# Laying one batch's attention as a row of ticks between half-steps of another batch's MoE

## The chip, the cores and the metric

The kernel runs on one core of a Trainium2 chip. The metric is the device time of one execution in microseconds (us). The kernel before takes 290.18 us (median of three runs, 288.84 to 292.52). A profile of one execution gives a span of 288.6 us from the first to the last instruction; all windows and rows below come from it.

## The reference: what is computed

Eight batches (B), eight heads, 576 positions (S), head width 64. First an attention without a score matrix, then a mixture of experts in which a whole batch goes to one expert:

```python
q_s = softmax(q, axis=-1)                     # over the 64 columns of a row
k_s = softmax(k, axis=2)                      # over the 576 positions
kv  = einsum('bhsd,bhse->bhde', k_s, v)       # 64 x 64 per head
x   = einsum('bhsd,bhde->bhse', q_s, kv)      # then laid as B x S x 512
pooled = x.mean(axis=1); logits = pooled @ w_gate       # one row of 8 per batch
e = argmax(logits); gate = softmax(logits)[e]
out[b] = gate * (relu(x[b] @ w1[e]) @ w2[e])  # 512 -> 1024 -> 512
```

The exact softmaxes subtract the maximum and add 1e-9 to the sum; the kernel leaves both out for q and k, whose values are small. With the inputs used here the eight batches choose the experts 2, 3, 3, 1, 3, 3, 4 and 6.

## The kernel before

Each batch is worked on in two halves of four heads (n = 0 to 15). A half loads q, k and v (three tiles of 128 x 1152, 576 KB each), takes exps on ScalarE, casts v on GpSimd, sums and scales q, and then runs through TensorE in the steps KV, T (twice), X (twice). After two halves the batch has its input X to the MoE, kept transposed in `xt`, and a gate step picks the expert and starts the transfer of its weights into one of five slots, unless another slot holds them already. Later a "fetch" on VectorE copies the slot that holds the weights into the batch's own slot (onto itself where they were just loaded).

```python
BUFS = {"mm": 3, "ht": 1, "kv": 2, "t": 1, "x": 1}     # PSUM: eight banks of 128 x 512 fp32
def bank(tag):
    return psum.tile([128, 512], FP32, name=tag, tag=tag, bufs=BUFS[tag])

def prepare_half(n):                       # all at one place in the order
    nc.scalar.activation(out=eq, in_=q, func=Exp)
    nc.scalar.activation(out=ek, in_=k, func=Exp)
    nc.gpsimd.tensor_copy(out=va, in_=v)
    nc.vector.tensor_reduce(out=qs, in_=eq, op=add)
    nc.vector.reciprocal(out=qsi, in_=qs)
    eng = nc.vector if n < 4 else nc.gpsimd
    eng.tensor_tensor(out=eq, in0=eq, in1=qsi, op=mult)
    load_half(n + 3)

def attention(b):                          # a generator: 12 steps per batch
    for i in range(2):
        kps = [bank("kv") for g in range(2)]
        # ... KV: 18 matmuls into kps[g][:, 0:129]; VectorE scales them into kvs[g]
        yield
        for g in range(2):
            tp = bank("t")                 # batch 0: "mm" for g == 1
            # ... T: nine transposes of eq into tp
            nc.vector.tensor_copy(out=qt, in_=tp)
            yield
        for g in range(2):
            px, pxt = bank("x"), kps[g][:, 192:256]       # 512 and 64 columns
            # ... X: one matmul into each
            nc.vector.tensor_tensor_reduce(out=xt[:, c, 0:512], in0=px, ..., accum_out=pooled)
            nc.vector.tensor_tensor_reduce(out=xt[:, c, 512:576], in0=pxt, ..., accum_out=pooled)
            yield
    # ... gate: pooled @ w_gate into bank("x"), argmax, DMAs of w1 and w2 on GpSimd's queue
    nc.vector.tensor_single_scalar(out=nmx, in_=mx8[:, 0:1], scalar=-1.0, op=mult)
    nc.scalar.activation(out=ex, in_=zz, func=Exp, bias=nmx, accum_out=sm)
    yield
    # ... VectorE: gt = 1 / sm, hl = gt in two fp16 parts; TensorE spreads hl over 128 partitions
    yield

def moe(b):                                # a generator: 13 units
    for fc in range(8):
        # ... H: 4 matmuls of 512 columns into bank("mm"), 4 of 64 into "ht"; ScalarE: ReLU to hsb
        yield
    for st in range(4):
        # ... O: 8 matmuls of 512 columns into bank("mm"); ScalarE: osb = gate * po; DMA out
        yield
    # ... tail: 16 matmuls of 256 columns
    yield
```

The order of the instructions on each engine is the order of the program. Attention is run ahead: 18 attention steps before the first MoE, then 1.25 steps after every MoE unit, and `fetch(b-1)` of w1 and of w2 stand at steps 6 and 8 of batch b.

Of the kernel before, what the change touches and what calls it, by code (L numbers as in the profile page):

```python
# [9 lines left out]
FP32 = mybir.dt.float32  # L10
FP16 = mybir.dt.float16
U32 = mybir.dt.uint32
AF = mybir.ActivationFunctionType
ALU = mybir.AluOpType
# [5 lines left out]
def kernel(  # L20
# [40 lines left out]
    BUFS = {"mm": 3, "ht": 1, "kv": 2, "t": 1, "x": 1}  # L61

    def bank(tag):
        return psum.tile([128, 512], FP32, name=tag, tag=tag, bufs=BUFS[tag])

# [39 lines left out]
    def pair_src(t, b, i):  # L105

        return t[b].rearrange("(i n g) (p j) d -> i (g p) n (j d)", i=2, n=2, p=64)[i]
# [5 lines left out]
    def load_half(n):  # L113
        if n >= 2 * B:
            return
        b, i = divmod(n, 2)
        ins[n] = {}
        for name, t in (("q", q), ("k", k), ("v", v)):
            x = in_pool.tile([128, 2, J * Dh], FP32, name=f"{name}_in")
            nc.sync.dma_start(out=x, in_=pair_src(t, b, i))  # L120
            ins[n][name] = x.rearrange("p n (j d) -> p n j d", j=J)

    def prepare_half(n):
        t = ins.pop(n)
        eq = e_pool.tile([128, J, 2, Dh], FP16, name="eq")
        nc.scalar.activation(out=eq.rearrange("p j n d -> p n j d"), in_=t["q"], func=AF.Exp)  # L126
        ek = e_pool.tile([128, J, 2, Dh], FP16, name="ek")
        nc.scalar.activation(out=ek.rearrange("p j n d -> p n j d"), in_=t["k"], func=AF.Exp)  # L128
        va = v_aug[n % NVB]
        nc.gpsimd.tensor_copy(out=va[:, :, 1:].rearrange("p j (n d) -> p n j d", n=2), in_=t["v"])  # L130
        qs = stat.tile([128, J, 2], FP32, name="qs")
        nc.vector.tensor_reduce(out=qs, in_=eq, op=ALU.add, axis=AX.X)  # L132
        qsi = stat.tile([128, J, 2], FP32, name="qsi")
        nc.vector.reciprocal(out=qsi, in_=qs)  # L134
        eng = nc.vector if n < 4 else nc.gpsimd
        eng.tensor_tensor(  # L136
            out=eq, in0=eq, in1=qsi.unsqueeze(3).to_broadcast([128, J, 2, Dh]), op=ALU.mult,
        )
        halves[n] = (eq, ek, va)
        load_half(n + 3)  # L140

    def attention(b):
        roomy = b == 0
        xt = xt_pool.tile([128, ND, S], FP16, name="xt")
        pooled = gat_pool.tile([128, ND], FP32, name="pooled")
        for i in range(2):
            eq, ek, va = halves.pop(2 * b + i)
            kps = [bank("kv") for g in range(2)]
            for j in range(J):
                for g in range(2):  # L150
                    r = slice(64 * g, 64 * g + 64)
                    nc.tensor.matmul(  # L152
                        kps[g][:, 0:129], lhsT=ek[r, j], rhs=va[r, j],
                        start=(j == 0), stop=(j == J - 1),
                    )
            kvs = []
            for g in range(2):
                icv = kv_pool.tile([128, 1], FP32, name="icv")
                nc.vector.reciprocal(out=icv, in_=kps[g][:, 0:1])  # L159
                kv = kv_pool.tile([128, 128], FP16, name="kv")  # L160
                nc.vector.scalar_tensor_tensor(
                    out=kv, in0=kps[g][:, 1:129], scalar=icv, in1=blkmask, op0=ALU.mult, op1=ALU.mult,
                )
                kvs.append(kv)
            yield
            qts = []
            for g in range(2):
                r = slice(64 * g, 64 * g + 64)
                tp = bank("mm" if roomy and g == 1 else "t").bitcast(FP16)
                for j in range(J):  # L170
                    nc.tensor.transpose(  # L171
                        out=tp[:, 64 * j:64 * j + 64], in_=eq[r, j], identity=ident[r, r],
                    )
                qt = qt_pool.tile([128, S], FP16, name="qt")
                nc.vector.tensor_copy(out=qt, in_=tp[:, 0:S])  # L175
                qts.append(qt)
                yield
            for g in range(2):
                c = 2 * i + g
                px = bank("mm" if roomy and g == 1 else "x")  # L180
                pxt = kps[g][:, 192:256]
                nc.tensor.matmul(px, lhsT=kvs[g], rhs=qts[g][:, 0:SM], start=True, stop=True)  # L182
                nc.tensor.matmul(pxt, lhsT=kvs[g], rhs=qts[g][:, SM:S], start=True, stop=True)  # L183
                nc.vector.tensor_tensor_reduce(  # L184
                    out=xt[:, c, 0:SM], in0=px, in1=ones_f32.to_broadcast([128, SM]),
                    scale=1.0, scalar=0.0, op0=ALU.mult, op1=ALU.add, accum_out=pooled[:, c:c + 1],
                )
                nc.vector.tensor_tensor_reduce(
                    out=xt[:, c, SM:S], in0=pxt, in1=ones_f32.to_broadcast([128, ST]),
                    scale=1.0, scalar=pooled[:, c:c + 1], op0=ALU.mult, op1=ALU.add,  # L190
                    accum_out=pooled[:, c:c + 1],
                )
                yield
# [13 lines left out]
        cond, sidx = None, None  # L207
# [40 lines left out]
        seqs[b] = [xt, None, sidx]  # L248
        nmx = gat_pool.tile([1, 1], FP32, name="nmx")
        nc.vector.tensor_single_scalar(out=nmx, in_=mx8[:, 0:1], scalar=-1.0, op=ALU.mult)  # L250
        ex = gat_pool.tile([1, E], FP32, name="ex")
        sm = gat_pool.tile([1, 1], FP32, name="sm")
        nc.scalar.activation(out=ex, in_=zz, func=AF.Exp, bias=nmx, accum_out=sm)
        yield
        gt = gat_pool.tile([1, 1], FP32, name="gt")
        nc.vector.reciprocal(out=gt, in_=sm)

        hl = gat_pool.tile([1, 2], FP16, name="hl")
        nc.vector.tensor_copy(out=hl[:, 0:1], in_=gt)
        nc.vector.tensor_scalar(  # L260
            out=hl[:, 1:2], in0=hl[:, 0:1], scalar1=gt, scalar2=-2048.0, op0=ALU.subtract, op1=ALU.mult
        )
        pb = bank("x")
        nc.tensor.matmul(pb[:, 0:2], lhsT=ones_row, rhs=hl, start=True, stop=True)
# [3 lines left out]
        seqs[b][1] = gate  # L268
        yield

    def fetch(b, w_all):

        sidx = seqs[b][2]
        if sidx is None:
            return
        s_val = nc.values_load(
            sidx[0:1, 0:1], engines=[ET.DVE], min_val=0, max_val=NS - 1,
            skip_runtime_bounds_check_because=IN_RANGE,
        )
        nc.vector.tensor_copy(  # L280
            out=w_all[:, b % NS], in_=w_all[:, ds(s_val, 1)].rearrange("p o c f -> p (o c) f")
        )

    def moe(b):
        xt, gate, _ = seqs[b]
# [22 lines left out]
        for st in range(4):  # L308
            po = bank("mm")
            for fc in range(NF):  # L310
                nc.tensor.matmul(  # L311
                    po, lhsT=hsb[:, fc, st * 128:st * 128 + 128], rhs=w2_sb[:, fc, :],
                    start=(fc == 0), stop=(fc == NF - 1),
                )
            osb = o_pool.tile([128, D], FP32, name="osb")
            nc.scalar.mul(osb, po, gate)  # L316
            for jj in range(2):
                nc.sync.dma_start(out=out_p[b, :, 2 * st + jj], in_=osb[64 * jj:64 * jj + 64])
            yield
# [16 lines left out]

    NA = 12
    att = {}
    pos = [0]
    prepared = [0]  # L340

    def att_step():

        if pos[0] >= NA * B:
            return False
        b, s = divmod(pos[0], NA)
        half_now = min(2 * b + (1 if s >= 1 else 0) + (1 if s >= 6 else 0), 2 * B - 1)
        while prepared[0] <= half_now:
            prepare_half(prepared[0])
            prepared[0] += 1  # L350
        if b not in att:
            att[b] = attention(b)
        if b and s == 6:
            fetch(b - 1, w1_all)
        if b and s == 8:
            fetch(b - 1, w2_all)
        next(att[b])
        pos[0] += 1
        return True

    for n in range(3):
        load_half(n)
        if n == 0:
            load_wg()
    with tc.manual_schedule(engines={ET.PE, ET.DVE, ET.Activation, ET.Pool, ET.SP}):
        for _ in range(NA + 6):
            att_step()
        owed = 0.0
        for b in range(B):
            for m, _ in enumerate(moe(b)):  # L370
                owed = min(owed + 1.25, NA * (b + 3) - pos[0])
                while owed >= 1.0:
                    att_step()
                    owed -= 1.0
                if m == 10 and b + 1 < B:
                    while pos[0] < NA * (b + 2):
                        att_step()
            if b == B - 2:
                fetch(B - 1, w1_all)
                fetch(B - 1, w2_all)  # L380
# [30 lines left out]
```

The softmax here doesn't subtract the row's maximum and nothing guards it: scores larger than these inputs give would overflow.

## Time and profile before

| what | value |
|---|---|
| median time, span of the profile | 290.18 us, 288.6 us |
| first MoE matmul | 39.94 us |
| the last two MoEs, with no attention inside | 15.85 and 15.91 us |
| granted TensorE clock, mean over the span | 0.887 |
| DMA queue 1 (inputs, outputs), share of 16 engines | 40.3% |
| DMA queue 0 (weights), share of 16 engines | 22.7% |

A row of a group or of the order of time names the source line, the engine, the operation, and output <- input by the program's names, with partitions x elements and type. "x9" is a count. In the order of time the first number is the start and the second the length in us; a bracket holds the idle time of that engine just before and what ended it. A row of waits names the engine and line that waited, what it waited for, the total in us, the number of times and the longest. PEld is the load of TensorE's stationary operand, which overlaps the matmuls. Line L171 is the transposes, L175 the copy of their result, L182 X, L184 its reading, L264 the spreading of the gate, L280 the slot copy, L293 and L311 the two MoE matmuls, L132 the sum for q.

### The profile page before, as it was taken

To read this page: it belongs to the slowest core of one execution; us is meant where nothing else is said; L and a number is where in the kernel's file an instruction comes from. 1 tells how busy PE (TensorE), PEld (TensorE's weight loads), DVE (VectorE), ACT (ScalarE), POOL (GpSimd) and SP (SyncE) were. 2 spreads that over 40 slices of the span, in tenths; PEclk is the share of its full clock that TensorE was granted. 3 is DMA by queue.
4 is the path that set the end of the run, shared out by engine and by line. 5 is a ranking of instruction groups with operands and counts; after the bars stand their busy time and mean duration, and the time that the engine had idled before them with its cause. 6 is when DMAs were issued, how large, how long until landed. Compare 5 with 4: busy or idle time off the path is not lost.

```text
span 288.6 us, 4585 instructions
## 1 busy us (share of the span) xinstructions
PE 197.5 (68%) x1608; PEld 102.6 (36%) x1608; DVE 132.5 (46%) x416; ACT 105.0 (36%) x161; POOL 68.0 (24%) x89
## 2 busy tenths in 40 slices
PE   0242376667577296673796649959289688899992
PEld 0230243433344142441353323534134444454541
DVE  2677745553756842448514574143841447211000
ACT  4330214255045222541334511453124523454641
POOL 1310742371114205332014020140206200500000
PEclk9999997999599787995997966986759959999999
DMA  7999899499917726997156261410007950798324
GB/s 234 395 391 392 225 242 313 115 191 294 374 44 242 249 53 130 189 313 267 38 121 213 74 214 31 98 36 2 0 0 141 219 98 0 146 222 164 93 49 116
DMA packets 28791, 48.55 MB, mean 168 GB/s; under 512 B 3168, under 2 KB 10336, under 8 KB 28768
## 3 DMA queue, kind: packets, MB, share of 16 engines
q1 hardware_dynamic: 19456, 37.76, 40.3%
q0 software_dynamic: 8736, 10.49, 22.7%
q8 instruction: 12, 0.20, 0.3%
q10 hardware_dynamic: 576, 0.02, 0.1%
q14 instruction: 11, 0.09, 0.1%
HBM read 61.88 MB, written 9.44 MB: 247 GB/s over the span
## 4 chain that ended last, share of the span: by engine, by line
PE 42%; DVE 12%; ACT 4%; issue 2%; DVEq 0%; ACTq 0%
PE mm L311 17%; PE mm L293 15%; DVE w_all L280 3%; DVE qs L132 3%; ACT eq L126 3%; PE mm L324 2%; DVE xt L184 2%; PE x L182 2%; PE kv L152 2%; PE t L171 2%; PE ht L298 2%; DVE qt L175 1%; DVE qsi L134 1%; ACT hsb L302 1%; PE x L196 0%
## 5 line engine op out<-in xcount | busy, mean ns | idle before, releaser
L293 PE MATMUL mm<-xt,w_all 128*128 128x512 f16 x256 | 75.0, 424 | 0.0
L302 ACT ACTIVATE hsb<-mm 128x512 f16<-128x512 f32 x64 | 38.1, 595 | 85.2 <-PE mm L293 85.2
L311 PE MATMUL mm<-w_all,hsb 128*128 128x512 f16 x256 | 66.9, 416 | 0.0
L171 PE MATMUL t<-ident,eq 64*128 64x64 f16 x270 | 15.2, 207 | 45.8 <-DVE qt L175 45.8
L316 ACT ACTIVATE osb<-mm,gate 128x512 f32<-128x512 f32 x32 | 22.0, 686 | 54.8 <-PE mm L311 33.8
L136 POOL TENSOR_TENSOR eq<-eq,qsi 128x1152 f16<-128x1152 f16 x12 | 25.4, 2115 | 68.7 <-DVE qsi L134 64.1
L311 PEld LDWEIGHTS <-hsb 128*128 128x128 f16 x256 | 25.1, 105 | 36.9 <-issue 14.4
L241 POOL DMA_DIRECT2D w_all<-in_moe_w_dram x36 | 15.2, 427 | 96.1 <-DVE hl L260 51.9
L280 DVE COPY w_all<-w_all 128x4096 f16 x14 | 25.0, 1788 | 18.7 <-DMA w_all<-in_moe_w_dram 14.8
L132 DVE TENSOR_REDUCE qs<-eq 128x18 f32<-128x1152 f16 x16 | 21.6, 1350 | 23.7 <-ACT eq L126 23.7
L293 PEld LDWEIGHTS <-w_all 128*128 128x128 f16 x256 | 21.8, 105 | 27.8 <-issue 12.9
L171 PEld LDWEIGHTS <-eq 64*128 64x128 f16 x288 | 13.3, 106 | 47.7 <-issue 46.6
L184 DVE CUSTOM_DVE_ANT_0 xt<-x,ones_f 128x512 f16<-128x512 f32 x30 | 20.7, 690 | 17.1 <-PE kv L183 13.1
L182 PE MATMUL x<-qt,kv 128*128 128x512 f16 x30 | 15.2, 508 | 14.8 <-DVE qt L175 7.6
L298 PEld LDWEIGHTS <-w_all 128*128 128x128 f16 x256 | 17.8, 105 | 18.3 <-issue 5.7
L152 PE MATMUL kv<-va,ek 64*128 64x129 f16 x288 | 15.1, 252 | 12.9 <-POOL va L130 10.9
L159 DVE RECIPROCAL icv<-kv 128x1 f32<-128x1 f32 x32 | 5.2, 163 | 38.8 <-PE kv L152 38.8
L130 POOL CAST va<-v_in 128x1152 f16<-128x1152 f32 x16 | 18.9, 1183 | 13.6 <-DMA v_in<-in_v_dram 13.4
L126 ACT ACTIVATE eq<-q_in 128x1152 f16<-128x1152 f32 x16 | 18.5, 1156 | 4.7 <-DMA q_in<-in_q_dram 4.7
L298 PE MATMUL ht<-xt,w_all 128*128 128x64 f16 x256 | 19.3, 201 | 0.0
L128 ACT ACTIVATE ek<-k_in 128x1152 f16<-128x1152 f32 x16 | 18.5, 1154 | 0.8 <-DMA k_in<-in_k_dram 0.8
L152 PEld LDWEIGHTS <-ek 64*128 64x128 f16 x288 | 11.2, 110 | 17.6 <-ACT ek L128 8.9
(58 smaller groups left out, 134.0 us busy)
## 6 DMA issues: line engine op xcount, KB each, us to landing
q_in<-in_q_dram SPq DMA_DIRECT2D x16, 576.0 KB, 6.8
k_in<-in_k_dram SPq DMA_DIRECT2D x16, 576.0 KB, 7.0
v_in<-in_v_dram SPq DMA_DIRECT2D x16, 576.0 KB, 7.7
w_all<-in_moe_w_dram POOLq DMA_DIRECT2D x16, 512.0 KB
out_dram<-osb SPq DMA_DIRECT2D x64, 128.0 KB, 2.4
w_all<-in_moe_w_dram POOLq DMA_DIRECT2D x28, 256.0 KB
w_all<-in_moe_w_dram POOLq DMA_DIRECT2D x8, 128.0 KB
out_dram<-osb_t SPq DMA_DIRECT2D x16, 64.0 KB, 2.9
```

The costliest lines, as they stand in the source:

```text
L126: nc.scalar.activation(out=eq.rearrange("p j n d -> p n j d"), in_=t["q"], func=AF.Exp)
L132: nc.vector.tensor_reduce(out=qs, in_=eq, op=ALU.add, axis=AX.X)
L136: eng.tensor_tensor(out=eq, in0=eq, in1=qsi.unsqueeze(3).to_broadcast([128, J, 2, Dh]), op=ALU.mult,)
L152: nc.tensor.matmul(kps[g][:, 0:129], lhsT=ek[r, j], rhs=va[r, j], start=(j == 0), stop=(j == J - 1),)
L171: nc.tensor.transpose(out=tp[:, 64 * j:64 * j + 64], in_=eq[r, j], identity=ident[r, r],)
L184: nc.vector.tensor_tensor_reduce(out=xt[:, c, 0:SM], in0=px, in1=ones_f32.to_broadcast([128, SM]), scale=1.0, scalar=0.0, op0=ALU.mult, op ...
L280: nc.vector.tensor_copy(out=w_all[:, b % NS], in_=w_all[:, ds(s_val, 1)].rearrange("p o c f -> p (o c) f"))
L293: nc.tensor.matmul(phm, lhsT=w1_sb[:, c, fsl], rhs=xt[:, c, 0:SM], start=(c == 0), stop=(c == ND - 1),)
L298: nc.tensor.matmul(pht[:, fc * ST:(fc + 1) * ST], lhsT=w1_sb[:, c, fsl], rhs=xt[:, c, SM:S], start=(fc == 0 and c == 0), stop=(fc == NF - ...
L302: nc.scalar.activation(out=hsb[:, fc, 0:SM], in_=phm, func=AF.Relu)
L311: nc.tensor.matmul(po, lhsT=hsb[:, fc, st * 128:st * 128 + 128], rhs=w2_sb[:, fc, :], start=(fc == 0), stop=(fc == NF - 1),)
L316: nc.scalar.mul(osb, po, gate)
```

## The change: what it does and what it is for

The two generators that were mixed by a count of owed steps become a table: every attention operation gets a tick, and the MoE moves a clock on as its units go by, so that the distance between an operation and its user is set by hand. The O units of the MoE are halved, which gives 17 places for attention in place of 13. The exps, the scaling of q and the slot copies are no longer tied to one place; the slot copies come in quarters. The transposes lose their own bank: they go into the free upper columns of the two KV banks. The freed bank makes the X tile two banks wide, so that X's 576 columns are read in one instruction. In batch 0 ScalarE takes the transposes' copies and every second reading of X. A few single-element operations of the gate move from VectorE to GpSimd, the scaling of q of halves 2 and 3 too, and the first input loads are reordered. The gate step of batch b moves to the start of the MoE of batch b-1. It is for keeping TensorE supplied from queues that no longer stand in each other's way.

```diff
-    BUFS = {"mm": 3, "ht": 1, "kv": 2, "t": 1, "x": 1}
+    BUFS = {"mm": 3, "ht": 1, "kv": 2, "x": 1}
-        return psum.tile([128, 512], FP32, ...)
+        return psum.tile([128, 1024 if tag == "x" else 512], FP32, ...)
 # --- transposes
-                tp = bank("mm" if roomy and g == 1 else "t").bitcast(FP16)
+        tp = kps[g].bitcast(FP16)[:, 448:448 + S]
+        if n < 2:
+            nc.scalar.copy(qt, tp)
+        else:
+            nc.vector.tensor_copy(out=qt, in_=tp)
 # --- X: one reading of 576 columns
-                pxt = kps[g][:, 192:256]
+        nc.tensor.matmul(px[:, SM:S], lhsT=kvs[g], rhs=qts[g][:, SM:S], start=True, stop=True)
+        if b == 0 and g == 1:
+            nc.scalar.activation(out=xt[:, c, :], in_=px[:, 0:S], func=AF.Copy, accum_out=...)
+        else:
+            nc.vector.tensor_tensor_reduce(out=xt[:, c, :], in0=px[:, 0:S], ...)
 # --- gate
-        nc.vector.tensor_single_scalar(out=nmx, in_=mx8[:, 0:1], ...)
+        nc.gpsimd.tensor_single_scalar(out=nmx, in_=seqs[b]["mx8"][:, 0:1], ...)
-        nc.vector.tensor_copy(out=hl[:, 0:1], in_=gt)
-        nc.vector.tensor_scalar(out=hl[:, 1:2], ...)
+        nc.gpsimd.tensor_copy(out=hl[:, 0:1], in_=gt)
+        nc.gpsimd.tensor_scalar(out=hl[:, 1:2], ...)
 # --- slot copies in quarters
+    def fetch(b, w_all, part):
+        half = w_all.shape[2] // 2
+        cs = slice(part * half, (part + 1) * half)
 # --- MoE, O units
+                if fc == 3:
+                    yield
 # --- the ticks (... = cut)
+    for b in range(B):
+        for i in range(2):
+            n, t0 = 2 * b + i, NA * b + 5 * i
+            at(t0, kv_step, n)
+            for g in range(2):
+                at(t0 + 1 + g, t_step, n, g)
+                at(t0 + 3 + g, x_step, n, g)
+        at(NA * b + 10, gate_step, b)
+        at(NA * b + 11, gate_exp, b)
+        at(NA * b + 12, gate_split, b)
+        at(NA * b + 14, gate_spread, b)
+        if b:
+            for part in range(2):
+                at(NA * (b + 1) + 6 + part, fetch, b, w1_all, part)
+                at(NA * (b + 1) + 8 + part, fetch, b, w2_all, part)
+    for n in range(2 * B):
+        t0 = NA * (n // 2) + 5 * (n % 2)
+        early = n < 2
+        at(t0 - 6, exp_q, n)
+        at(t0 - 6, cast_v, n)
+        at(t0 - 5, exp_k, n)
+        if n + 3 < 2 * B:
+            at(t0 - 5, load, n + 3)
+        at(t0 - (6 if early else 4), scale_q, n, nc.vector if early else nc.gpsimd)
+    load(0, "qk"); load(1, "q"); load(0, "v"); load(1, "kv"); load_wg(); load(2)
+        tick = NA + 6.0
+        run_ticks(tick)
+        for b in range(B):
+            units = 17
+            for m, _ in enumerate(moe(b)):
+                goal = NA * (b + 2) + 10
+                left = units - m
+                tick = min(tick + max(0.7, (goal - tick) / left), NA * (b + 3))
+                run_ticks(tick)
```

On TensorE the order of a middle MoE becomes (H and O4 are a hidden unit and half an output unit, K the KV matmuls, G and B the gate's two steps): H G H H K H H T H B T H H X O4 X O4 K O8 T O4 T O8 X O4 X O-tail. GpSimd's order around a gate is: the issue of the weight DMAs, nmx, the cast of v, hl.

## The prediction
> **What bounds the kernel now.** I read the engine totals first, then the MoE stages by window, then TensorE's own waits, then the order of time around the longest wait.
>
> ```profile
> PE 197.5 (68%) x1608; PEld 102.6 (36%) x1608; DVE 132.5 (46%) x416; ACT 105.0 (36%) x161; POOL 68.0 (24%) x89
> ```
>
> No engine is full. TensorE leads, so the question is what its 91 idle us wait for, and whether its busy time is all work. The windows below run from the first hidden-layer matmul of one batch's MoE to that of the next (found in the order of time; columns are window, length, busy time and instructions of PE, PEld, DVE, ACT, POOL, granted clock, DMA share, GB/s):
>
> ```profile
> 0.00:39.94 39.94, 11.74 (x147) 8.20 (x148) 24.68 (x77) 10.76 (x11) 13.53 (x24) 1.00 0.97 319
> 39.94:78.00 38.06, 26.41 (x222) 13.80 (x221) 19.96 (x60) 14.27 (x21) 12.56 (x11) 0.89 0.99 252
> 78.00:115.38 37.38, 25.98 (x215) 13.20 (x214) 20.60 (x76) 13.14 (x22) 10.54 (x16) 0.84 0.51 153
> 115.38:148.60 33.22, 22.88 (x202) 12.12 (x203) 17.07 (x51) 12.76 (x20) 8.10 (x12) 0.90 0.73 188
> 148.60:185.13 36.53, 26.85 (x203) 13.27 (x203) 17.07 (x51) 12.87 (x20) 6.76 (x10) 0.81 0.43 130
> 185.13:222.76 37.63, 27.96 (x202) 13.65 (x203) 17.07 (x51) 12.87 (x20) 9.43 (x10) 0.77 0.18 37
> 222.76:251.84 29.08, 24.04 (x202) 12.57 (x203) 13.63 (x49) 10.87 (x18) 6.95 (x8) 0.88 0.61 116
> 251.84:267.69 15.85, 15.85 (x115) 7.91 (x114) 2.45 (x2) 8.49 (x14) 0.13 (x1) 1.00 0.95 184
> ```
>
> The last line is an MoE with no attention inside: 15.85 us, no idle time. The six above it carry attention of a later batch and last 29 to 38 us. At full clock that attention costs TensorE about 4.5 us per batch, from single rows in the order of time: two KV groups at 0.65, four transpose groups at 0.43, four X pairs at 0.25, gate matmuls 0.44. So 20.4 us would do; the stage at 148.6 takes 36.5. Of the excess of 16.1, 9.7 is idle (36.53 - 26.85) and 6.4 is matmuls at a lower clock (26.85 - 20.4). TensorE's waits in that stage add up to the same 9.7:
>
> ```profile
> PE t L171 <- DVE qt L175: 7.9, 2, 5.7
> PE x L182 <- DVE pooled L184: 1.5, 2, 0.7
> PE x L264 <- DVE hl L260: 0.3, 1, 0.3
> ```
>
> The second transpose group waits because the one bank "t" is not yet copied out. The order of time shows what VectorE did instead:
>
> ```profile
> 201.59 1.35 DVE L132 TENSOR_REDUCE qs<-eq 128x18 f32<-128x1152 f16 x1 [2.18 <-ACT eq L126]
> 203.05 0.27 DVE L134 RECIPROCAL qsi<-qs 128x18 f32<-128x18 f32 x1
> 203.73 2.95 DVE L280 COPY w_all<-w_all 128x4096 f16 x1 [0.42 <-DVE qsi L134]
> 206.61 0.44 DVE L175 COPY qt<-t 128x576 f16<-128x576 f16 x1
> 207.10 0.64 PE L171 MATMUL t<-ident,eq 64*128 64x64 f16 x9 [5.66 <-DVE qt L175]
> 207.67 1.89 PE L293 MATMUL mm<-xt,w_all 128*128 128x512 f16 x4
> ```
>
> VectorE stands in program order: it waits for an exp, sums it, copies a weight slot, and only then takes the 0.44 us copy that TensorE needs. Afterwards four matmuls take 1.89 us, where the same four take 1.04 in an undisturbed stretch. **The bound is TensorE's queue held by VectorE's order, and the clock lost after it.** In the first 78 us there is a second bound: DMA shares of 0.97 and 0.99.
>
> [...]the 128x4096 slot copy took 2.95 us beside GpSimd's q scaling (203.49 to 205.61) and 1.23 us alone at 208.34.[...]
>
> **The change part by part.**
>
> (1) Transposes go into the upper columns of the KV banks (one bank per group), X gets a two-bank tile. The two transposes of a half no longer share a bank, so the wait of 7.9 us per stage goes. A group now waits only for the read of its own KV sums.
>
> (2) X is read in one pass of 576 columns. Removed per batch: four tail passes of 0.284 + 0.084 and their gaps, 1.5 us of VectorE. The tile is still single: X0's reading is about 0.2 latency + 0.76 + 0.1, and one half-step of 0.87 us (half of 1.73 for eight matmuls) lies between X0 and X1, so each pair still waits 0.2 to 0.3: 0.5 per stage in place of 1.5.
>
> (3) Slot copies in four quarters: 128x2048 should take about 0.65 us alone, 1.5 beside GpSimd. They are now spread, none stands ahead of a copy by more than one piece. VectorE keeps about 15 us per batch (132.5 / 8 - 1.5), below 20.4: not the bound, but in the second half of a stage its queue from KV reading to the last X reading is, in the new program's order, 1.3 + 1.6 + 0.44 + 0.9 + 0.44 + 0.9 + 0.77 + 1.62 + 0.9 + 0.77 = 9.6 us, against 8.8 for TensorE up to the gate matmuls (O8, T, O4, T, O8, X, O4, X, tail, one H). The gate waits about 1 us.
>
> (4) The gate moves to the start of the next MoE, and nmx and hl move to GpSimd, **behind the issue of the weight DMAs** in GpSimd's order. ScalarE's order is: two ReLUs, gate exp, exp of q, ReLU. In the trace, at batch 2 (no weights needed), the gate matmuls end at 80.74 and the last skipped DMA at 85.37, so nmx is ready 4.9 us after the gate and ScalarE's third ReLU ends at about 4.9 + 0.1 + 0.3 + 1.16 + 0.6 = 7.1. TensorE can run H, H, K, H, H, T until 5.1 and then has no free "mm" bank: a **new wait of about 2 to 2.3 us per batch**. Where weights are fetched (batch 6: gate 215.32, last issue ends 222.61) nmx comes 7.4 us after the gate: 4.5 us. The inputs choose experts 2, 3, 3, 1, 3, 3, 4, 6, so batches 0, 1, 3, 6, 7 fetch.
>
> (5) In the head, q of the second half loads third, so V of the first lands one transfer (1.5 us) later, but batch 0's evictions go to ScalarE and the second q scaling no longer follows the KV step. Walking the queues with the rows of before, gate 0 falls near 23 us instead of 27.3. Its gate spread stands among the next batch's transposes behind about 6.4 us of DMA issue on GpSimd, so most of this is given back: first MoE matmul at about 38.4 instead of 39.94.
>
> Sums. A full stage: 20.4 + gate wait 1.0 + ReLU wait 2.3 + X 0.5[...] = **26**; with fresh weights 28.5, and in batch 3's stage 3 to 4 more, as the slot copy asks for weights about 15 us after the gate and they take 3 to 6 us to issue and 13 to land (22.7% of 288.6 us for five sets), beside input loads. First MoE: weights of batch 1 are held by DMA (at 5.45 us per half, 40.3% of 288.6 over inputs and outputs, nine halves and two sets are 75 us), so the second MoE starts near 74 instead of 78. Then 74 + 26 + 32 + 26 + 26 + 30.5 + 20.5 (the MoE with gate 7: 15.9 + 4.6) + 16 + 5 for the end = 256 us of span. The measured time of before is 1.6 us above its span: 257.6, said as **257 us**.
>
> **The rivals.** *Clock and waits heal fully:* if nmx is early enough and stalls under 2 us leave the clock high (after 1.64 us of idle at 83.57 four matmuls took 1.04), stages take 22 and the time is near 238. For it: three mm banks of slack. Against it: GpSimd's order is fixed. *The ScalarE wait takes the place of the old one:* if the held ReLUs also hold KV reading (the gate's reciprocal on VectorE stands before it)[...], stages take 30 to 32 and the time is 275 to 285. For it: 2.24 us of idle at 191.62 was followed by slow matmuls. *DMA bounds:* queues 0 and 1 took 63% of the span, 183 us; if slot copies wait for late weights, VectorE holds everything again, in three stages: 265 to 270. A plain loss would need waits of more than 16 us in every stage; nothing in the orders gives that.
>
> **Range and chances.** The five full stages carry most of the doubt, 22 to 30 us each, +-4 us x 5 = 20 if all agree; the head +-4. Eight in ten: 240 to 276. Under 284.4 (faster by 2%) I put 0.93, within 2% 0.04, slower 0.03.
>
> **What would show it.** Right: the transposes' wait for qt is gone from TensorE's waits; stages near 26 us; TensorE waits most for ReLUs just after the gate matmuls (hidden-layer matmuls released by ScalarE), ScalarE's gate exp waits for GpSimd's nmx; longest where weights are fetched; granted clock over 0.9. Wrong: stages of 22 us with no ReLU wait (part 4 too dear), or TensorE waiting for KV reads, qt or X readings through VectorE's slot copies, or the first MoE's end still at 78.

## The result, and the profile after

The changed kernel takes 249.2 us (median of four runs, 247.9 to 253.23) against 289.51 us for the kernel before, a ratio of 0.858 with a 95% interval of 0.848 to 0.868. The prediction said 257, with 240 to 276 as its range.

All views of "after" below are from a further run of the same code: 249.68 us (249.14 to 251.55), ratio 0.862 (0.848 to 0.875), span of the profile 247.8 us. First the totals of its page:

```profile
PE 183.3 (74%) x1608; PEld 96.4 (39%) x1608; DVE 108.4 (44%) x332; ACT 106.7 (43%) x169; POOL 78.3 (32%) x115
```

TensorE executes the same 1608 matmuls but is busy 183.3 us instead of 197.5: 14.2 us of the gain are the same matmuls in less time, at a mean granted clock of 0.941 in place of 0.887. Its idle time falls from 91.1 to 64.5 us. The two changes add up to the 40.8 us by which the span shrank. Where they fall is read from the windows between first hidden-layer matmuls (columns as in the prediction: window, length, busy time of PE, PEld, DVE, ACT, POOL, granted clock, DMA share, GB/s):

```profile
0.00:43.19 43.19, 12.11 (x147) 8.26 (x148) 17.03 (x52) 14.27 (x19) 18.19 (x29) 1.00 1.01 307
43.19:76.02 32.83, 25.04 (x225) 12.80 (x224) 17.32 (x51) 14.24 (x21) 11.09 (x13) 0.90 0.93 250
...
101.02:128.27 27.25, 22.68 (x203) 11.82 (x201) 13.98 (x43) 12.50 (x20) 11.35 (x13) 0.94 1.00 250
128.27:151.96 23.69, 21.18 (x204) 11.24 (x202) 13.77 (x43) 12.50 (x20) 7.59 (x13) 1.00 0.66 204
...
175.30:203.15 27.85, 23.47 (x204) 12.17 (x202) 13.99 (x44) 10.57 (x18) 10.24 (x12) 0.88 0.66 119
203.15:226.80 23.65, 19.11 (x123) 9.15 (x122) 4.58 (x18) 8.52 (x16) 4.70 (x9) 0.86 0.73 129
```

Two groups of stages stand apart. The stage at 128.27, whose gate fetches no weights, lasts 23.69 us at clock 1.00; so does its neighbour at 151.96 (23.34 us). The stages whose gate fetches (43.19, 101.02, 175.30, 203.15) are longer, and their clock is lower (0.86 to 0.94). The one at 76.02 lies between: it fetches nothing and lasts 25.00 us at clock 0.93. TensorE's waits in the stage at 128.27, the counterpart of the waits shown of before:

```profile
PE kv L174 <- POOL va L129: 1.6, 1, 1.6
PE mm L310 <- ACT hsb L319: 0.5, 1, 0.5
PE x L206 <- DVE pooled L197: 0.4, 1, 0.4
```

The 7.9 us for qt are gone; 2.5 us of waiting remain in place of 9.7. Line 174 is the transposes, which now write into the banks named kv, L310 the hidden-layer matmuls, L319 their ReLU, L206 the gate matmuls, L197 the reading of X, L129 the cast of v. The same view of the whole span, now for all engines (the time before the first MoE included):

```profile
ACT ex L265 <- POOL nmx L262: 47.6, 8, 12.9
...
PE kv L174 <- POOL va L129: 29.6, 7, 12.5
```

ScalarE's gate exp waits for GpSimd's nmx, 47.6 us in all. The second line names the cast of v as what released TensorE. The order of time around the gate of batch 6, whose weights are fetched, says otherwise:

```profile
176.85 0.34 PE L206 MATMUL x<-wg_sb,pooled 128*1 128x8 f32 x8 [0.39 <-DVE pooled L197]
...
179.85 2.78 POOL L251 DMA_DIRECT2D w_all<-in_moe_w_dram  x4 [1.75 <-DVE hist L233]
182.82 1.51 POOL L257 DMA_DIRECT2D w_all<-in_moe_w_dram  x2 [0.19 <-issue]
184.35 0.22 POOL L262 TENSOR_SCALAR nmx<-mx 1x1 f32<-1x1 f32 x1
184.61 0.30 ACT L265 ACTIVATE ex<-zz,nmx 1x8 f32<-1x8 f32 x1 [5.81 <-POOL nmx L262]
185.04 0.15 DVE L270 RECIPROCAL gt<-sm 1x1 f32<-1x1 f32 x1 [6.17 <-ACT ex L265]
185.29 0.35 DVE L163 SCALAR_TENSOR_TENSOR kv<-kv,icv,blkmask 128x128 f16<-128x128 f32 x1
185.69 0.63 PE L174 MATMUL kv<-ident,eq 64*128 64x64 f16 x9 [3.73 <-POOL va L129]
186.58 1.86 PE L310 MATMUL mm<-xt,w_all 128*128 128x512 f16 x4 [0.26 <-ACT hsb L319]
```

The gate matmuls are done at 177.2. GpSimd issues six weight DMAs, the last until 184.33, and only then negates one number. ScalarE has stood 5.81 us at its exp, VectorE 6.17 us at its reciprocal, and the reading of the KV sums (L163) stands behind that reciprocal in VectorE's order. The transposes write into the bank that this reading must free; they start when it ends. Then the matmuls are slower: four take 1.86 us, where four took 1.04 before the stall (at 179.83). In the page's slice from 185.85 to 192.05 us the granted clock is 5 tenths.

### The profile page after: what moved, and what is told of

Read it like the earlier page. It is cut to its first block, busy times and chain, and to the rows that moved or that the text cites. A ratio compares the mean times of both kernels' runs of the same rounds, so it can differ in the third digit from the quotient of the medians.

```text
span 251.6 us, 4504 instructions
## 1 busy us (share of the span) xinstructions
PE 187.0 (74%) x1608; PEld 97.5 (39%) x1608; DVE 108.4 (43%) x332; ACT 107.0 (43%) x169; POOL 78.5 (31%) x115
## 5 line engine op out<-in xcount | busy, mean ns | idle before, releaser
L310 PE MATMUL mm<-xt,w_all 128*128 128x512 f16 x256 | 74.4, 423 | 6.8 <-ACT hsb L319 6.8
L328 PE MATMUL mm<-w_all,hsb 128*128 128x512 f16 x256 | 64.0, 389 | 0.0
L144 POOL TENSOR_TENSOR eq<-eq,qsi 128x1152 f16<-128x1152 f16 x14 | 30.9, 2207 | 83.8 <-DVE qsi L143 72.2
L319 ACT ACTIVATE hsb<-mm 128x512 f16<-128x512 f32 x64 | 36.6, 589 | 36.4 <-PE mm L310 36.4
L174 PE MATMUL kv<-ident,eq 64*128 64x64 f16 x288 | 16.2, 209 | 31.6 <-POOL va L129 30.1
L197 DVE CUSTOM_DVE_ANT_0 xt<-x,ones_f 128x576 f16<-128x576 f32 x30 | 22.6, 754 | 27.9 <-PE x L193 27.9
L310 PEld LDWEIGHTS <-w_all 128*128 128x128 f16 x256 | 22.2, 104 | 29.5 <-issue 15.6
L328 PEld LDWEIGHTS <-hsb 128*128 128x128 f16 x256 | 22.4, 99 | 25.4 <-issue 1.9
L251 POOL DMA_DIRECT2D w_all<-in_moe_w_dram x36 | 15.5, 437 | 31.9 <-issue 18.9
L265 ACT ACTIVATE ex<-zz,nmx 1x8 f32<-1x8 f32 x8 | 2.4, 299 | 48.1 <-POOL nmx L262 48.1
L129 POOL CAST va<-v_in 128x1152 f16<-128x1152 f32 x16 | 18.5, 1155 | 13.5 <-DMA v_in<-in_v_dram 13.5
L296 DVE COPY w_all<-w_all 128x2048 f16 x28 | 19.1, 682 | 8.2 <-DMA w_all<-in_moe_w_dram 5.3
L154 PE MATMUL kv<-va,ek 64*128 64x129 f16 x288 | 13.1, 241 | 11.4 <-POOL va L129 11.4
L192 PE MATMUL x<-qt,kv 128*128 128x512 f16 x32 | 13.6, 426 | 5.8 <-DVE pooled L197 2.7
```

What stands on the lines that cost most here:

```text
L144: eng.tensor_tensor(out=eq, in0=eq, in1=qsi.unsqueeze(3).to_broadcast([128, J, 2, Dh]), op=ALU.mult,)
L174: nc.tensor.transpose(out=tp[:, 64 * j:64 * j + 64], in_=eq[r, j], identity=ident[r, r])
L197: nc.vector.tensor_tensor_reduce(out=xt[:, c, :], in0=px[:, 0:S], in1=ones_f32.to_broadcast([128, S]), scale=1.0, scalar=0.0, op0=ALU.mult ...
L296: nc.vector.tensor_copy(out=w_all[:, b % NS, cs], in_=w_all[:, ds(seqs[b]["src"], 1), cs].rearrange("p o c f -> p (o c) f"),)
L310: nc.tensor.matmul(phm, lhsT=w1_sb[:, c, fsl], rhs=xt[:, c, 0:SM], start=(c == 0), stop=(c == ND - 1),)
L319: nc.scalar.activation(out=hsb[:, fc, 0:SM], in_=phm, func=AF.Relu)
```

## The experiments

The theory was: **the remaining loss is GpSimd's order around the gate, one number behind the issue of the weight DMAs.** Rivals: the weights' DMA itself bounds these stages; or the cast of v does, as the profile's name for the releaser suggests. Besides, the change's parts were separated. Ratios are to the kernel before, with 95% intervals. e1 to e4 start from the changed kernel, e5 from the kernel before, and e6 to e11 from the changed kernel with e2's edit.

**The changed kernel once more** (no edit).

> The changed kernel once more, unchanged, as the base for the runs beside it. Expected 248 to 250 us, the wait chain of the gate as in its first profile: about 1.3 to 1.7 us of TensorE idle at the transposes after a gate whose weights are there already, 3.7 us where weights are fetched, 12.6 us in the head.

Measured: the numbers above.

**e1: nmx on VectorE.**

```diff
-        nc.gpsimd.tensor_single_scalar(out=nmx, in_=seqs[b]["mx8"][:, 0:1], ...)
+        nc.vector.tensor_single_scalar(out=nmx, in_=seqs[b]["mx8"][:, 0:1], ...)
```

> Only nmx (one element, the negated maximum of the gate's logits) goes back to VectorE; hl stays on GpSimd. Theory A, nmx stands behind the issue of the weight DMAs in GpSimd's order and holds ScalarE's gate exp, VectorE's reciprocal behind it and the KV reading behind that: ScalarE's wait of 48 us for nmx falls under 12 us, the transposes' waits in the middle stages go (0 to 0.5 us each), the middle stages come to 21.5 to 23 us and the MoE with gate 7 to about 18; in the head hl still stands behind the DMA issue, so the first MoE matmul stays near 42 to 43. Time 230 to 236 us. Theory B, the loss comes from where the gate stands (start of the MoE, three mm banks to run on) and not from who computes nmx: the ReLU and transpose waits stay within 1 us of what they are, time 245 or more.

Measured: 240.72 us (239.87 to 241.13), ratio 0.828 (0.817 to 0.840). The order of time at the same gate, in e1:

```profile
178.25 0.43 PE L174 MATMUL kv<-ident,eq 64*128 64x64 f16 x9
...
180.67 1.18 POOL L129 CAST va<-v_in 128x1152 f16<-128x1152 f32 x1
...
182.06 0.31 POOL L273 TENSOR_SCALAR hl<-hl,gt 1x1 f16<-1x1 f16 x1
182.42 0.16 PE L281 MATMUL x<-hl,ones_row 1*128 1x2 f16 x1 [2.66 <-POOL hl L273]
```

The transposes run at 178.25, before the cast of v, which starts at 180.67. So they never needed that cast, and the releaser named in the changed kernel was something that happened to end at the same time. The rival "cast of v" falls with this. About 9 us are gained, but less than expected: the next number behind the DMA issue, hl, now holds TensorE at the gate's spread (24.3 us in seven waits over the span, 10.9 of it before the first MoE), and VectorE's copies wait 13.8 us for weights.

**e2: nmx and hl on VectorE.** As e1, and:

```diff
-        nc.gpsimd.tensor_copy(out=hl[:, 0:1], in_=gt)
-        nc.gpsimd.tensor_scalar(out=hl[:, 1:2], ...)
+        nc.vector.tensor_copy(out=hl[:, 0:1], in_=gt)
+        nc.vector.tensor_scalar(out=hl[:, 1:2], ...)
```

> nmx and both hl operations go back to VectorE, where the kernel before has them. Theory A: as in the run with nmx alone for the middle stages (21.5 to 23 us), and the head gains too, as the gate's spreading no longer waits behind the DMA issue; the KV step before the first MoE then waits for the cast of v, which still stands behind it, so the first MoE matmul comes near 38.5. Time 216 to 228 us. If DMA takes over (183 us of DMA work must fit), the stage of batch 0 stays over 33 us with VectorE's slot copies waiting for weights, and the time is 228 to 234. Theory B: 245 or more.

Measured: 234.49 us (233.09 to 238.21), ratio 0.804 (0.788 to 0.821). It lies just above the 228 to 234 us expected for the case that DMA takes over. Two neighbouring stages, then VectorE's and TensorE's longest waits in the second of them (all from an execution of e2 that took 236.71 us, 1.6% above its fastest; L296 is the slot copy, L192 X):

```profile
77.90:99.21 21.31, 21.31 (x203) 11.15 (x202) 13.11 (x44) 12.76 (x20) 6.36 (x10) 0.98 0.48 142
99.21:132.75 33.54, 22.32 (x204) 11.54 (x202) 15.15 (x48) 12.63 (x20) 11.34 (x11) 0.85 0.93 256
```

```profile
DVE w_all L296 <- DMA w_all<-in_moe_w_dram: 13.0, 2, 9.2
...
PE x L192 <- DVE pooled L197: 10.2, 1, 10.2
```

The first stage has no idle time at all. The second, which fetches, got *longer* than in the changed kernel (33.54 against 27.25): without the stalls VectorE reaches the slot copies before the weights have landed, waits 13.0 us there, and the readings of X stand behind it. In e7 below the stage's copies wait 10.0 us, so this is no accident of one profile. In the changed kernel the same stage shows no wait for weights. The first weight DMA and the next load of q, first in the changed kernel, then in e2, show one reason:

```profile
105.55 2.78 POOL L251 DMA_DIRECT2D w_all<-in_moe_w_dram  x4 [1.74 <-DVE hist L233]
111.78 0.37 SPq L119 DMA_DIRECT2D q_in<-in_q_dram  x1
```

```profile
103.73 2.77 POOL L251 DMA_DIRECT2D w_all<-in_moe_w_dram  x4 [1.72 <-DVE hl L272]
104.33 0.37 SPq L119 DMA_DIRECT2D q_in<-in_q_dram  x1
```

An input load waits for the exp that reads the old tile (7.9 us in the changed kernel's stage; the exp runs from 110.60 to 111.75, the load is issued at 111.78), and this exp stands behind the gate's exp on ScalarE. So the stall held back not only the copies but also the loads: 6.2 us lay between the weight DMA and the load of q, now 0.6. The first half of w2 was copied without a wait 18.9 us after the first weight DMA (at 124.42); in e2 the copy had to wait until 25.2 us after it (128.91). Whether the loads beside them slow the weights is what e6 tries. The rival "DMA bounds" was hidden, not absent.

**e3: the old PSUM layout under the new order** (a bank "t" for the transposes, X in one bank, its tail in a KV bank, two readings, all on VectorE).

```diff
-    BUFS = {"mm": 3, "ht": 1, "kv": 2, "x": 1}
+    BUFS = {"mm": 3, "ht": 1, "kv": 2, "t": 1, "x": 1}
-        tp = kps[g].bitcast(FP16)[:, 448:448 + S]
+        tp = bank("t").bitcast(FP16)[:, 0:S]
 # ... and x_step as in the kernel before
```

> The changed kernel's ticks with the PSUM layout of before: transposes share one bank t, X is 512 columns in one bank and 64 in the KV bank, read in two passes on VectorE (in batch 0 too). Theory 1, the row of ticks alone frees the queues, since a copy of a transpose group now stands right behind it in VectorE's order: middle stages within 1.5 us of the changed kernel's, time 250 to 256 us. Theory 2, the second bank for the transposes is what removes the wait of 7.9 us per stage: that wait returns at 4 us or more per stage, time 265 to 285 us.

Measured: 256.27 us (255.36 to 257.43), ratio 0.882 (0.868 to 0.896). So the new order alone (all of the change but the banks and the reading of X) gives about 34 us, and these two 6.6 us more on top of it (256.27 - 249.68). TensorE's longest wait in e3 over the whole span, and what is left of the transposes' wait for qt:

```profile
PE mm L313 <- ACT hsb L322: 18.5, 6, 4.5
...
PE t L174 <- DVE qt L179: 0.6, 1, 0.6
```

In the kernel before, the same wait costs TensorE 45.8 us over the span, as the row of the transposes in its page shows (busy time and mean ns, then the idle time before them and what ended it):

```profile
L171 PE MATMUL t<-ident,eq 64*128 64x64 f16 x270 | 15.2, 207 | 45.8 <-DVE qt L175 45.8
```

The new order removes nearly all of this even with the one old bank. In e3 the transposes have a bank that the KV sums don't share and pass, and the same chain from GpSimd stops TensorE at the ReLUs. This is the place that the prediction named. In the changed kernel the transposes stop first, because they share a bank with the KV sums.

**e4: slot copies whole instead of in two parts of each weight.**

```diff
-            for part in range(2):
-                at(NA * (b + 1) + 6 + part, fetch, b, w1_all, part)
-                at(NA * (b + 1) + 8 + part, fetch, b, w2_all, part)
+            at(NA * (b + 1) + 6, fetch, b, w1_all, 0)       # the whole tensor
+            at(NA * (b + 1) + 8, fetch, b, w2_all, 0)
```

> The changed kernel with the slot copies whole again (one of w1 at tick 6, one of w2 at tick 8 of the next batch's row) in place of quarters. If the quarters matter, VectorE's queue in the second half of a stage gets 0.6 us longer pieces ahead of the transposes' copies and of X's reading, and a copy of 128x4096 may fall beside GpSimd's scaling (2.95 us as before): middle stages 0.5 to 2 us longer, time 252 to 260 us. If they don't, because TensorE reaches the X steps later than VectorE either way: within 1.5 us of the changed kernel.

Measured: 250.76 us (248.39 to 251.88), ratio 0.863 (0.854 to 0.871): no difference to be seen. The 14 whole copies take 1.22 to 1.23 us each, none of them 2.95 us as in the kernel before beside GpSimd's q scaling. At these ticks none meets that scaling (2.12 us in the mean of 14; 2.37 in the changed kernel where a quarter ran beside it), so their place is enough to keep them short, and cutting them gives nothing on top.

**e5: the order of before with the new banks** (transposes into the KV banks, X in two banks and one reading; all operations where the kernel before has them).

```diff
-    BUFS = {"mm": 3, "ht": 1, "kv": 2, "t": 1, "x": 1}     # of the kernel before
+    BUFS = {"mm": 3, "ht": 1, "kv": 2, "x": 1}
-                tp = bank("mm" if roomy and g == 1 else "t").bitcast(FP16)
+                tp = kps[g].bitcast(FP16)[:, 448:448 + S]
 # ... and X in its two-bank tile, read once, on VectorE in batch 0 too
```

> The kernel before, in its own order, with the new PSUM layout alone: transposes in the upper columns of the KV banks, X in a two-bank tile read in one pass. If the shared bank was the cause of the wait of 7.9 us per stage, it goes and the time falls to 245 to 260 us. If VectorE's order was the cause, the wait only moves to the X step that needs the same late copy, one hidden unit or two (1 to 2 us) later: stages 32 to 35 us, time 270 to 284 us.

Measured: 265.48 us (265.03 to 265.97), ratio 0.915 (0.909 to 0.920), about 25 us less than before and between the two ranges expected. TensorE's longest wait in its stage at 137.62, 31.91 us long:

```profile
PE x L181 <- DVE qt L175: 5.0, 2, 4.2
```

The wait for qt has moved from the second transpose to the X matmul that reads qt, and shrunk from 7.9 to 5.0 us (over the whole span from 45.8 to 32.6): VectorE's order still makes qt late, but TensorE has more work that it can do before. Banks alone give 25 us, order alone 34, both 40: the two parts remove the same wait in different ways, and their gains do not add.

**e6 to e11** build on e2 and ask how the wait for weights is to be removed. *e6* loads inputs two halves ahead instead of three, so that fewer inputs are in flight beside the weights. *e7* adds an earlier cast of v of the odd halves.

```diff
-        if n + 3 < 2 * B:                                # e6, e7, e9, e11
-            at(t0 - 5, load, n + 3)
+        if n >= 1 and n + 2 < 2 * B:
+            at(t0 - 5, load, n + 2)
-        at(t0 - 6, cast_v, n)                            # e7 only
+        at(t0 - (8 if n % 2 and n > 1 else 6), cast_v, n)
```

> nmx and hl on VectorE as in the earlier run, and every input load from half 3 on is issued one half later (two halves ahead in place of three). If the stages of batches 0 and 2 (40.2 and 33.5 us there) are held by weights that share DMA with input loads, VectorE's slot copies wait less: 10 us in place of 27 over both stages, stages of 34 to 36 and 25 to 29 us, time 220 to 229 us. If the weights' own transfer time is what holds them (13 us at full rate after an issue of 4.5), the time stays within 3 us of 234.5. If inputs now come late, ScalarE waits for q and k and the time rises.

> As the run with late loads, and the cast of v of every second half stands ahead of the gate step in GpSimd's order, so that the KV step before the first MoE does not wait for the issue of 10 weight DMAs. The head falls from 37.7 to 34 to 36.5 us, where the first weights' arrival holds it (the ninth weight DMA was issued at 34.55 when an earlier one had landed). Time 1 to 3 us under the run with late loads; if DMA holds the stage of batch 0, its end doesn't move and the time is within 1 us.

Measured: e6 229.84 us (228.74 to 233.55), ratio 0.790 (0.785 to 0.795); e7 233.8 us (231.37 to 235.6), ratio 0.807 (0.800 to 0.813). Late loads give about 5 us, no more: in the stages of batches 0 and 2 VectorE's copies still wait 9.7 and 10.0 us for weights in e7, against 14.4 and 13.0 in e2, where e6's expectation had 10 for both together. In e7 the first MoE starts at 35.11 (in e6 at 38.40), but its stage ends at 74.15 all the same (35.11 + 39.04; in e6 at 73.86), since it waits for weights. Here an earlier start in front of a transfer was worth nothing. Why e7 came out 4 us slower than e6 stays open.

*e8* (on e2) and *e9* (on e6) move the copies later instead: w1 by two ticks, w2 by four.

```diff
-                at(NA * (b + 1) + 6 + part, fetch, b, w1_all, part)
-                at(NA * (b + 1) + 8 + part, fetch, b, w2_all, part)
+                at(NA * (b + 1) + 8 + part, fetch, b, w1_all, part)
+                at(NA * (b + 1) + 12 + part, fetch, b, w2_all, part)
```

In these two, w2 is copied after the next gate has issued its weights; where that gate overwrites the source slot the copy takes the new weights, so that batch 5 is computed with the w2 of batch 6. Size and number of operations are the same.

> nmx and hl on VectorE, loads three halves ahead as in the changed kernel, and the slot copies stand later in VectorE's order: w1 two ticks later (8 and 9), w2 four ticks later (12 and 13, inside the next MoE, which needs w2 only from its ninth unit on). In the run with nmx and hl on VectorE the copies of batches 1 and 3 waited 14.4 and 13.0 us for weights and held the readings of X behind them. If it is the copy's place and not DMA's rate that costs, those stages fall from 40.2 and 33.5 us to about 29 to 33 and 22 to 26, time 214 to 224 us. If DMA's rate costs (weights can't be there earlier beside the input loads), VectorE stands at the copies as long, only later: time 228 to 236.

> As the run with late copies, and the loads two halves ahead as in the run with late loads. Stages of batches 0 and 2 at 28 to 32 and 22 to 25 us, all middle stages near 21.5; time 210 to 220 us, 2 to 6 below the run with late copies alone, as the weights of batches 1 and 3 share DMA with one input half less. If inputs come late, ScalarE waits for q and k and the time is above it.

Measured: 272.66 us, ratio 0.943 (0.935 to 0.951), and 269.16 us, ratio 0.930 (0.921 to 0.938): much slower than e2. VectorE's first wait in e9:

```profile
DVE w_all L296 <- DMA w_all<-in_moe_w_dram: 59.5, 6, 19.7
```

A copy that stands behind the next gate's DMA issue waits for that gate's weights as well. The wait of 19.7 us is that of w2 of batch 2, whose own gate fetched nothing. This direction fell, and it set the limit for the next one: behind the X readings, but ahead of the next gate.

*e10* (on e2) and *e11* (on e6) put w1 one tick later and both parts of w2 just ahead of the gate.

```diff
-                at(NA * (b + 1) + 6 + part, fetch, b, w1_all, part)
-                at(NA * (b + 1) + 8 + part, fetch, b, w2_all, part)
+                at(NA * (b + 1) + 7 + part, fetch, b, w1_all, part)
+                at(NA * (b + 1) + 9.5, fetch, b, w2_all, part)
```

> nmx and hl on VectorE, loads three halves ahead, and the slot copies still ahead of the next gate but as late as that allows: w1 at ticks 7 and 8, both of w2 at 9.5, behind the last reading of X and before the gate of the next batch. A copy then waits only for weights whose issue came before it. The readings of X no longer stand behind w2, and TensorE has the tail and five hidden units (about 6 us) before it needs VectorE again. If the place of the copies is what cost, the stages of batches 0 and 2 (40.2 and 33.5 us with the copies at 6 to 9) lose about 5 to 8 us each, time 219 to 227 us. If DMA's rate is what costs, the next stage gives back what these win: 230 to 236.

> The same with loads two halves ahead. Against the run with late loads (229.8 us): w1 of batches 1 and 3 waited 2.2 and 3.7 us there and w2 7.3 and 7.7 us; one tick and two and a half ticks later (about 1.3 us a tick) and with 6 us of TensorE work behind, 10 to 14 us of those 21 should go: time 216 to 222 us. If it stays at 227 or more, DMA's rate holds the chain and not the copies' place.

Measured: e10 229.13 us (228.38 to 230.94), ratio 0.793 (0.788 to 0.798). **e11 217.51 us (216.36 to 220.71), ratio 0.751 (0.746 to 0.755), which beats both kernels.** In e10 the stages of batches 0 and 2 fall from 40.19 and 33.54 us (e2) to 28.45 and 21.81, but the ones behind them rise from 21.31 and 21.20 to 28.25 and 29.04: the wait moves on to the next stage, as its expectation had it for the case that DMA's rate costs, and only part of it goes. In the stage at 116.33, 29.04 us long, the two copies of w2, just ahead of the gate in VectorE's order, hold VectorE until the weights land; the KV reading and then TensorE's transposes stand behind them:

```profile
DVE w_all L296 <- DMA w_all<-in_moe_w_dram: 6.6, 1, 6.6
PE kv L174 <- DVE kv L163: 5.8, 1, 5.8
```

With the loads two halves ahead as well, three stages of e11 one after the other:

```profile
63.73:89.76 26.03, 22.67 (x203) 11.84 (x202) 14.12 (x46) 12.65 (x20) 6.76 (x10) 0.93 0.68 224
89.76:111.58 21.82, 21.10 (x203) 11.23 (x202) 15.64 (x46) 12.51 (x20) 10.39 (x10) 1.00 1.10 276
111.58:133.75 22.17, 21.10 (x204) 11.23 (x202) 14.17 (x46) 12.50 (x20) 6.72 (x10) 1.00 0.77 250
```

The second and third stay within 1.1 us of TensorE's 21.1 us, and so do the two that follow (21.82 each). The stages of e10 that lasted 28.25 and 29.04 us are the first and third of these, 26.03 and 22.17. Either measure alone left 229 to 230 us, and together they remove 12 more. What is left in e11 is the head (37.68 us) and the first fetched weights (stage of 26.03 us).

## Why the prediction was right

The total was inside the range and the cause that the prediction gave for the remaining loss, the gate's number behind the DMA issue on GpSimd, is shown by e1 and e2. But that the sum was right to 8 us is partly luck: without their signs the differences below add up to 24 us. The stages (us; predicted as the text has them, the first MoE from 38.4 to 74):

| stretch | predicted | measured | difference |
|---|---|---|---|
| head, to the first MoE matmul | 38.4 | 43.2 | +4.8 |
| first MoE | 35.6 | 32.8 | -2.8 |
| second (gate 2 fetches nothing) | 26 | 25.0 | -1.0 |
| third (gate 3 fetches) | 32 | 27.3 | -4.7 |
| fourth, fifth (fetch nothing) | 26, 26 | 23.7, 23.3 | -5.0 together |
| sixth (gate 6 fetches) | 30.5 | 27.9 | -2.6 |
| seventh (gate 7 fetches) | 20.5 | 23.7 | +3.2 |
| last MoE and end | 16 + 5 | 15.9 + 5.1 | 0 |

**Step 1, banks: the wait goes as said, but the shared bank was not its only cause.** The transposes' wait for qt is gone. e5 shows that the banks alone take 25 us away and leave 5.0 us of the wait in a stage, at X; e3 shows that the order alone removes it at the transposes with the old bank in place (0.6 us over the span).

**Step 2, X: right in direction, too dear.** Each X pair was to wait 0.2 to 0.3 us, 0.5 per stage. In the five full stages no X matmul is among the waits.

**Step 3, slot copies and the gate's wait: mis-sized.** A quarter takes 0.65 to 0.70 us, as said; the five that ran into GpSimd's q scaling took 0.65 too, not 1.5; it was the scaling that took longer there, 2.37 us in place of 2.12. But the gate's wait for the last X reading is 0.4 us, not 1.0, and e4 shows that the cutting into quarters gives nothing.

**Step 4, nmx behind the DMA issue: right, and its times right to 0.4 us.** nmx was to be ready 4.9 us after a gate that fetches nothing and 7.4 after one that fetches; from the end of the gate matmuls to the end of nmx it took 5.3 (130.17 to 135.47) and 7.4 (177.19 to 184.57). The wait was to be 2 to 2.3 us and 4.5 us. Measured: 1.6 + 0.5 = 2.1 at 128.27, and 4.5 in the seventh stage, all of it at the ReLUs. But where TensorE stops was only half right: with attention beside it, it stops mostly at the transposes, since VectorE's reciprocal holds the KV reading. The waits at the ReLUs, said to be the largest, are 6.8 us over the whole span, those at the transposes behind the first MoE matmul 17.1 (29.6 - 12.5). That is the first half of the second rival. Its second half, 30 us and more for a full stage, did not come.

**Slow matmuls after a stall: the part that was most wrong in the middle.** The prediction's full stage of 26 us lies 1.8 us above the four terms that it names (20.4 + 1.0 + 2.3 + 0.5 = 24.2). This rest, for matmuls at a lower clock after a stall, was the author's guess; no trace of before was shown for its size. Measured, such a loss is missing in the fourth and fifth stage, 1.5 us in the second and third, 2.3 in the sixth and 2.7 in the seventh. The fourth stage is 21.2 of busy time + 0.4 + 2.1 = 23.7, with nothing for the clock (1.00); at full clock the matmuls take 0.8 us more than the 20.4 that the prediction added up. In the seventh, 4.5 us of waiting made matmuls that take 16.44 us in e11, without a stall, into 19.11, which is 2.7 us more; in the sixth, busy time is 23.47 against 21.18 for the fourth, 2.3 us more. Slow matmuls follow all four stalls of 3.7 us and more in the MoEs (5.4, 3.70, 3.73 and 4.5 us). But the length of a stall alone does not decide what it costs. 3.70 + 0.5 us in the third stage cost 1.5 us (22.68 against 21.18), 3.73 + 0.3 us in the sixth 2.3 us; 1.6 + 0.5 us left the full clock in the fourth, while 1.3 + 0.6 us in the second was followed by four matmuls in 1.56 us and cost 1.5 us as well. What else decides it, no run here shows. So the first rival's condition, stalls under 2 us leave the clock high (an estimate between the stalls of 1.64 and 2.24 us that it names), was met in two stages of the three that fetch nothing. For the sixth stage the sum has 30.5 us, though the prediction's own terms for fresh weights give 28.5; it took 27.9.

**Weights, 3 to 4 us more in the third stage: wrong.** The changed kernel has no such wait there. The prediction added the stall and the wait for weights, though the stall delays the copies (the first came 19 us after the gate matmuls, not 15) and the input loads that share the DMA, and so gives the weights time. e2, with the stall taken away, shows the wait: 13.0 us.

**First MoE, held by DMA until about 74: the end is near (76.02), the reason is not shown.** The prediction let nine halves and two sets of weights, 75 us of DMA, pass before the second MoE. e10, with the loads as far ahead as in the changed kernel, starts it at 66.27 (37.82 + 28.45): with the copies placed later, not all of these transfers have to be over by then.

**Step 5, the head: wrong.** Gate 0 came as said (23.1 us; ScalarE's copies took 0.63 to 0.65 us), but the first MoE at 43.2, not 38.4. "About 6.4 us of DMA issue" was to stand before the gate's spread. The order of time in the head shows what was missed:

```profile
25.40 4.99 POOL L251 DMA_DIRECT2D w_all<-in_moe_w_dram  x8 [0.31 <-issue]
...
33.68 0.77 POOL L257 DMA_DIRECT2D w_all<-in_moe_w_dram  x1 [3.29 <-DMA w_all<-in_moe_w_dram]
...
35.70 0.23 POOL L262 TENSOR_SCALAR nmx<-mx 1x1 f32<-1x1 f32 x1
```

Issuing the ten weight DMAs of batch 0 takes 6.5 us (4.99 + 0.77 + 0.74), as said. But the ninth first waits 3.29 us for an earlier one to land, so the issue ends 10.3 us after it began. In the kernel before, whose gate is 4.2 us later, the ninth is issued at 34.48 us; here at 33.68, so of those 4.2 us only 0.8 are left there. nmx comes 12.6 us after the gate matmuls. With nmx and hl off GpSimd (e2) the first MoE starts at 37.71.

## What to carry to other kernels

An operation on one number belongs on no queue that issues DMAs ahead of it: here it held three engines (ScalarE 5.81, VectorE 6.17 and TensorE 3.73 us at gate 6), and moving three such operations took 15 us from a kernel of 250. Once a stall is removed, look at once for the transfer that it had been hiding and for the loads that it had held back beside it, and put the copy that waits for this transfer behind the work that doesn't need it, but ahead of the next issue into the same tile. When the profile names a releaser, see in the order of time whether the waiting work ever ran without it.

## What the runs showed of the hardware

- In the middle stages each weight DMA that GpSimd issues with a cast held its queue for 0.70 us (w1) or 0.75 us (w2): 2.78 us for four, 1.51 for two. GpSimd began nothing else meanwhile (from 179.85 to 184.35 in the stage of gate 6). Six DMAs skipped by their condition still took 2.4 us (132.74 to 135.14), against 4.5 for six that were issued (179.85 to 184.33), so skipping saved less than half.
- Of ten such DMAs in a row the first eight were issued without a wait (4.99 us), and the ninth stood 3.29 us until one had landed. What set this limit was not tried.
- After the 3.73 us stall the matmuls ran at about half rate for some 5.5 us: four in 1.86 us at 186.58, four in 1.89 us at 189.30, and only from 191.19 four in 1.03 us. After the stall of 3.70 us in the third stage the nine transposes still took 0.42 us, as in the fourth stage (0.42 at 136.58, clock 1.00); then four matmuls took 1.51 us (at 112.28) and the next nine transposes 0.66 us (at 114.05).
